# Linear attention, a gated network and a soft mixture of experts on one core: the gate's activation in one ScalarE instruction, and low parts moved from GpSimd to VectorE

## The chip, the cores and the metric

The kernel runs on one core of a Trainium2 chip. A core has a matrix engine (TensorE, PE in the profile, PEld for its weight loads), a vector engine (VectorE, DVE), an engine for functions and copies (ScalarE, ACT), a general engine (GpSimd, POOL) and a queue that issues DMAs (SyncE, SP). Each takes its instructions in order and waits for the others by semaphores. SBUF is the working memory on the chip, PSUM the banks that TensorE writes to. The metric is the device time of one execution in microseconds (us), the median of several runs.

## The reference

A softmax linear attention gives x of 2304 tokens by 512. A gated network with root-mean-square norm follows, and a mixture of eight experts, each weighted by a Sinkhorn-normalized router:

```python
def _moe_ref(x, w_gate, w_val, w_out, rms_g):          # 512 -> 1536 -> 512
    rms = np.sqrt(np.mean(x * x, axis=-1, keepdims=True) + 1e-06)
    xn = x / rms * rms_g
    g = xn @ w_gate
    silu = g * (1.0 / (1.0 + np.exp(-g)))
    val = xn @ w_val
    return (silu * val @ w_out).astype(np.float32)

def _moe2_ref(x, w_gate, w1, w2):                      # 8 experts, 512 -> 1024 -> 512
    ...                                                # P: 8 Sinkhorn steps over x @ w_gate
    for e in range(E):
        h = np.maximum(x @ w1[e], 0.0)
        out += P[:, e:e + 1] * (h @ w2[e])
```

All arrays are 32-bit floats. The change lies in the gated network alone.

## The kernel before

**Split operands.** TensorE multiplies with fp32r operands. To keep precision each operand is held as a high part (a cast by ScalarE) and a low part (value minus high part, a subtraction on VectorE or GpSimd), and a product is three matmuls: high by high, high by low, low by high (`mm3`). So every value that becomes an operand costs a cast and a subtraction, the "low part" of the change's title.

**Tiling.** The 2304 tokens are five blocks b: four of 512 and a fifth of 256 (the tails). The 1536 hidden features are twelve tiles f of 128. A product of one tile with one block accumulates in a PSUM bank.

**Features 0 to 5, plain products** (until about 330 us). `BLOCKS` is two groups: features 0 to 3 run while the attention of the later blocks is still computed, features 4 and 5 after that (from about 250 us). For each block and feature `m1_s1` forms g in a bank `pg`, then the activation, then val in a bank `pv`, multiplies (L835), and splits h (cast L837 on ScalarE, low part L838 on GpSimd). `m1_s2` multiplies h with w_out into four banks `y`, two features later in the queue, and `m1_evac` adds the banks to `acc` in SBUF (L868). The activation is silu(g) = g / (1 + exp(-g)) = 0.5 g (1 + tanh(g/2)): ScalarE forms tanh (L830), VectorE computes (tanh + 1) * g (L831), and the factor 0.5 is left to L864, L866, L868 and L1280, which take y out.

**Features 6 to 11, fast products** (about 330 to 570 us). Pairs of blocks, (0, 1) and (2, 3), are multiplied as a 2 by 2 block matrix with seven products instead of eight. `chain(f, p, gap, work)` does this for one feature f and one pair p: M1, M2, M6, M5, M7, M3, M4 in this order, three banks (x, y and then another y), sums out of them, two gates and two vals. First all features run with pair 0 (with `chain_tails` for the tails after each), then all with pair 1. `gap(k)` puts the products with w_out between (`y_gap`, added by L1280), `work(k)` other work: in pair 0 the next features' weights (`pass_tick`), in pair 1 work of the experts. In the order of the program, with the engine:

- M1 into x; ScalarE copies it to `m1` (L1202, tile `cm`). M6 is added into the same bank x, so M6 waits for that copy. `held` is emptied here: the split of the previous chain's second block is issued right after the copy of M1.
- M2 into y, M6 into x; VectorE m1 += y (L1210); ScalarE copies x to `u1` (L1211, `cu`; M7 waits for it) and forms tanh of m1 (L1212).
- M5 into a new y; VectorE (tanh + 1) * m1 (`silu`, L1188); ScalarE copies y to `m5` (L1219, `c5`; M3 waits for it).
- M7 into x; VectorE m5 += x (L1223; M4 waits for it).
- M3 into y; VectorE u1 += y (L1227); ScalarE tanh of u1 (L1229).
- M4 into x; VectorE th0 *= x (L1233), `silu` of u1 (L1188), split of the first block (cast L1192, low part on GpSimd L1193), th1 *= m5 (L1236); the split of the second block goes to `held`.

The tiles `cm`, `cu`, `c5` and the tails' `tt` take turns in three buffers (`c_tile`), so each waits for the last reader of the one before it in its buffer.

**Weights and sums of pairs.** `pass_tick` runs the JOBS: `convert` ("f", "o") turns raw weights, loaded as pairs of 32-bit words, into floats (L1006, L1007 on ScalarE, L1011, L1012, L1015 on VectorE), casts them (L1030, L1032), makes the low parts (L1033, L1043, L1054 on GpSimd) and for "f" the four sums of weight blocks (L1037 to L1041) with their split (L1044, L1047). It stores the result with a DMA of SP (L1050, L1056). `pair_sums` ("t") makes T1 to T4 of a pair of x blocks with their splits (cast L1081, low part L1085: T1 and T2 on GpSimd, T3 and T4 on VectorE); those of pair 1 are stored by SP (L1087). The tails' result of each feature is stored too (L2103), and SP's queue issues the next raw weights behind it.

The experts follow (from about 555 us): the same scheme with 32 units for each of three groups of tokens, TensorE busy nearly all the time. Their router needs one Exp on ScalarE (L936, at 594 us).

## Time and profile before

| what | value |
|---|---|
| median of 3 runs | 2021.13 us (2021.10 to 2022.15) |
| profiled execution, own time | 2021.51 us |
| its span, first to last instruction | 2019.7 us |
| TensorE busy | 1980.9 us, 98% |
| VectorE busy | 1664.8 us, 82% |
| ScalarE busy | 841.2 us, 42% |
| GpSimd busy | 196.8 us, 10% |
| mean granted TensorE clock | 0.999 |

The span is what the traces show; the device time has some 1.8 us around it. The page of a profile gives busy times and a chain of what ended last; the trace behind it can be asked for groups of instructions, for waits (who waited for whom and how long), for stretches of time and for the instructions in order. Matmuls are pipelined, one of 512 columns lasts about 0.39 us but the next starts 0.23 us after it, so TensorE's busy time is a union and a wait is what is left between.

### The profile page before, as it was taken

Reading aid. Unit: us, or ns where it says so; the run is one execution under the profiler, and the core shown is the slowest. Engines: PE = TensorE matmul, PEld = TensorE weight load, DVE = VectorE, ACT = ScalarE, POOL = GpSimd, SP = SyncE. Lnnn points to the kernel's source line nnn. Section 1 sums busy time; section 2 is a strip of 40 time slices with the busy share of each in tenths; the row PEclk is TensorE's granted clock in tenths of the full one; section 3 lists DMA queues with packets and bytes.
Section 4 is the critical chain, followed back from the end, with each engine's and each line's share of the span. In section 5 each row is a group of like instructions: output and inputs, shape, how many; then the busy total and the mean of one; then the engine's idle time right before and its main releaser. Section 6 shows DMA issues by size and latency. Waiting matters only on the chain.

```text
span 2019.7 us, 29232 instructions
## 1 busy us (share of the span) xinstructions
PE 1980.9 (98%) x10765; PEld 1836.3 (91%) x10765; DVE 1664.8 (82%) x3253; ACT 841.2 (42%) x1656; POOL 196.8 (10%) x189
## 2 busy tenths in 40 slices
PE   8899999899999999999999999999999999999999
PEld 7788887678778889998999999999999999999998
DVE  7865688867668878777778999999998899999898
ACT  5544434443445555454444333333334333333332
POOL 3532233321220000000000000000000000000000
PEclk9999999999999999999999999999999999999999
DMA  8410114468648888787978766777665777667663
GB/s 264 133 31 22 53 74 159 182 266 314 215 162 290 291 331 304 299 294 287 343 278 296 263 261 259 260 263 263 257 260 206 299 259 259 259 259 261 257 251 121
DMA packets 148838, 474.90 MB, mean 235 GB/s; under 512 B 12872, under 2 KB 77528, under 8 KB 144472
## 3 DMA queue, kind: packets, MB, share of 16 engines
q1 hardware_dynamic: 148424, 472.92, 64.1%
q8 instruction: 84, 1.38, 0.3%
q14 instruction: 58, 0.48, 0.1%
q10 hardware_dynamic: 272, 0.13, 0.0%
HBM read 331.50 MB, written 141.50 MB: 234 GB/s over the span
## 4 chain that ended last, share of the span: by engine, by line
PE 84%; DVE 8%; ACT 2%; issue 2%; POOL 1%; DMA 0%; ACTq 0%; SPq 0%; DVEq 0%; POOLq 0%
PE sb L1602 34%; PE sb L1848 13%; PE yb L1848 9%; PE yb L1637 4%; PE yb L1636 4%; PE yb L1635 4%; PE cx L1173 2%; PE pv L798 1%; PE pg L798 1%; PE cz L1173 1%; PE pg L800 1%; PE pv L799 1%; PE pv L800 1%; PE pg L799 1%; PE kv L455 1%
## 5 line engine op out<-in xcount | busy, mean ns | idle before, releaser
L1602 PE MATMUL sb<-op1T,u 128*128 128x384 f32 x1536 | 298.2, 335 | 0.1
L1865 DVE TENSOR_TENSOR acc<-sb,acc 128x384 f32<-128x384 f32 x480 | 260.6, 557 | 27.4 <-PE sb L1848 23.3
L1602 PEld LDWEIGHTS sb<-op1T,u 128*128 128x128 f32 x1536 | 269.3, 188 | 0.7 <-DVE op1T L1535 0.4
L1602 PE MATMUL sb<-op1B,u 128*128 128x384 f32 x1120 | 220.2, 334 | 0.0
L1602 PEld LDWEIGHTS sb<-op1B,u 128*128 128x128 f32 x1120 | 196.3, 188 | 0.4 <-DVE fx L1792 0.3
L1602 PE MATMUL sb<-op0T,u 128*128 128x384 f32 x768 | 149.9, 336 | 2.3 <-DVE cs L1677 1.1
L1602 PEld LDWEIGHTS sb<-op0T,u 128*128 128x128 f32 x768 | 135.5, 188 | 9.8 <-DVE cs L1677 2.6
L1792 DVE TENSOR_TENSOR fx<-mt,sb 128x384 f32<-128x384 f32 x128 | 71.0, 555 | 52.1 <-ACT mt L1796 31.2
L1602 PE MATMUL sb<-op0B,u 128*128 128x384 f32 x576 | 111.1, 336 | 0.0
L1848 PE MATMUL sb<-hc,u 128*128 128x384 f32 x504 | 104.6, 335 | 0.1
L1602 PEld LDWEIGHTS sb<-op0B,u 128*128 128x128 f32 x576 | 101.7, 188 | 2.8
L1848 PE MATMUL sb<-hd,u 128*128 128x384 f32 x492 | 102.1, 334 | 0.2 <-ACT acc L1863 0.2
L1848 PE MATMUL yb<-hd,u 128*128 128x384 f32 x426 | 96.7, 334 | 0.0
L1848 PEld LDWEIGHTS sb<-hc,u 128*128 128x128 f32 x504 | 88.7, 188 | 0.9 <-DVE acc L1865 0.6
L1848 PEld LDWEIGHTS sb<-hd,u 128*128 128x128 f32 x492 | 86.6, 188 | 0.7 <-ACT acc L1863 0.5
L1637 PE MATMUL yb<-u,hq 128*128 128x512 f32 x192 | 76.2, 397 | 0.7 <-DVE hq L1623 0.7
L1796 ACT COPY mt<-sb 128x384 f32<-128x384 f32 x64 | 30.8, 481 | 109.5 <-PE sb L1602 109.5
L1848 PEld LDWEIGHTS yb<-hd,u 128*128 128x128 f32 x426 | 75.9, 188 | 0.0
L1636 PE MATMUL yb<-u,hw 128*128 128x512 f32 x192 | 75.6, 394 | 0.0
L1637 PE MATMUL yb<-u,hw 128*128 128x512 f32 x192 | 75.6, 394 | 0.0
L1636 PE MATMUL yb<-u,hq 128*128 128x512 f32 x192 | 75.1, 391 | 0.0
L1747 DVE SCALAR_TENSOR_TENSOR fx<-fx,pb 128x384 f32<-128x384 f32 x128 | 71.3, 557 | 4.4
(472 smaller groups left out, 4613.0 us busy)
## 6 DMA issues: line engine op xcount, KB each, us to landing
u<-kept SPq DMA_DIRECT2D x256, 896.0 KB, 6.2
kept<-u SPq DMA_DIRECT2D x60, 896.0 KB, 6.0
kept<-u SPq DMA_DIRECT2D x58, 768.0 KB, 4.8
rw<-in_moe_w_dram SPq DMA_DIRECT2D x64, 512.0 KB, 5.9
pw<-w SPq DMA_DIRECT2D x12, 1024.0 KB, 4.4
w<-pw SPq DMA_DIRECT2D x12, 1024.0 KB, 7.7
kept<-u SPq DMA_DIRECT2D x58, 128.0 KB, 4.6
k<-in_k_dram SPq DMA_DIRECT2D x8, 512.0 KB, 4.4
```

Source lines behind the costliest of these rows:

```text
L798: nc.tensor.matmul(o, lhsT=w(0), rhs=xb[0], start=first, stop=False)
L799: nc.tensor.matmul(o, lhsT=w(0), rhs=xb[1], start=False, stop=False)
L800: nc.tensor.matmul(o, lhsT=w(1), rhs=xb[0], start=False, stop=last)
L1173: nc.tensor.matmul(bank, lhsT=Wf[f][wz][:, at], rhs=block_x(p, xname, xz, c), start=(start and c == 0 and j == 0), stop=(c == 1 and j == 2 ...
L1602: nc.tensor.matmul(bank[:, 0:NT], lhsT=w[wz][:, WI[wname], c, :], rhs=x[xz][c], start=(start and c == 0 and j == 0), stop=(c == 1 and j == 2),
L1635: nc.tensor.matmul(py, lhsT=h[:, 0, s], rhs=w2[0][:, d], start=(u == 0 and f == 0), stop=False)
L1636: nc.tensor.matmul(py, lhsT=h[:, 0, s], rhs=w2[1][:, d], start=False, stop=False)
L1637: nc.tensor.matmul(py, lhsT=h[:, 1, s], rhs=w2[0][:, d], start=False, stop=(u == UE - 1 and f == 1))
L1747: nc.vector.scalar_tensor_tensor(out=fb[name], in0=c, scalar=0.0, in1=pbc[g, e][z], op0=ALU.max, op1=ALU.mult,)
L1792: add = lambda o, a, b: nc.vector.tensor_tensor(out=o, in0=a, in1=b, op=ALU.add)
L1848: nc.tensor.matmul(bank[:, 0:NT], lhsT=w[wz][:, d], rhs=h[:, hz], start=(start and k == 0), stop=True, skip_group_check=True)
L1865: nc.vector.tensor_tensor(out=a, in0=bank[:, 0:NT], in1=a, op=ALU.add)
```

## The change

Three things. (a) From feature 4 on ScalarE computes Silu itself (one instruction in place of tanh on ScalarE and (tanh + 1) * g on VectorE); the factor 0.5 goes from L868 (features 4 and 5) and from L1280, which become plain sums. Features 0 to 3 keep the old form. (b) In `convert` of kind "f" the second low part (L1043) and in `pair_sums` the low parts of T1 and T2 (L1085) move from GpSimd to VectorE (`tt` is VectorE's tensor_tensor). (c) In `chain` the low part of the second block moves to VectorE; the first block's stays on GpSimd.

```diff
--- before.py
+++ after.py
@@ -827,10 +827,13 @@
         n = ntok(b)
         pg = s1_project("g", f, b, tick)
         th = tp.tile([P, 512], F32, tag="th", name=f"th{f}_{b}")
-        nc.scalar.activation(out=th[:, 0:n], in_=pg[:, 0:n], func=AF.Tanh, scale=0.5)
-        nc.vector.scalar_tensor_tensor(
-            out=th[:, 0:n], in0=th[:, 0:n], scalar=1.0, in1=pg[:, 0:n], op0=ALU.add, op1=ALU.mult
-        )
+        if f < BLOCKS[0][1]:
+            nc.scalar.activation(out=th[:, 0:n], in_=pg[:, 0:n], func=AF.Tanh, scale=0.5)
+            nc.vector.scalar_tensor_tensor(
+                out=th[:, 0:n], in0=th[:, 0:n], scalar=1.0, in1=pg[:, 0:n], op0=ALU.add, op1=ALU.mult
+            )
+        else:
+            nc.scalar.activation(out=th[:, 0:n], in_=pg[:, 0:n], func=AF.Silu)
         pv = s1_project("v", f, b, tick)
         nc.vector.tensor_tensor(out=th[:, 0:n], in0=th[:, 0:n], in1=pv[:, 0:n], op=ALU.mult)
         h = hp.tile([P, 2, 512], F32R, tag="h", name=f"h{f}_{b}")
@@ -865,9 +868,7 @@
             elif t == 0:
                 nc.vector.tensor_scalar(out=av[:, j, :], in0=py[j][:, 0:n], scalar1=0.5, scalar2=None, op0=ALU.mult)
             else:
-                nc.vector.scalar_tensor_tensor(
-                    out=av[:, j, :], in0=py[j][:, 0:n], scalar=0.5, in1=av[:, j, :], op0=ALU.mult, op1=ALU.add
-                )
+                nc.vector.tensor_tensor(out=av[:, j, :], in0=py[j][:, 0:n], in1=av[:, j, :], op=ALU.add)
 
     LX = {}
 
@@ -1040,7 +1041,7 @@
             tt(out=sums[:, 2], in0=a11, in1=a21, op=ALU.subtract)
             tt(out=sums[:, 3], in0=a12, in1=sums[:, 1], op=ALU.subtract)
             sums = sums.rearrange("p k n -> p (k n)")
-            nc.gpsimd.tensor_tensor(out=o[1][1], in0=mf[1], in1=o[0][1].bitcast(F32), op=ALU.subtract)
+            tt(out=o[1][1], in0=mf[1], in1=o[0][1].bitcast(F32), op=ALU.subtract)
             cp(out=W[0][:, 1024:2048], in_=sums)
             yield
             after()
@@ -1081,8 +1082,7 @@
                 cp(out=home(name, 0), in_=v)
 
             def low(name, v):
-                eng = nc.gpsimd if name in ("T1", "T2") else nc.vector
-                eng.tensor_tensor(out=home(name, 1), in0=v, in1=f32(home(name, 0)), op=ALU.subtract)
+                tt(out=home(name, 1), in0=v, in1=f32(home(name, 0)), op=ALU.subtract)
                 if job[1] and name != "T1":
                     nc.sync.dma_start(out=t_view(pt[name])[:, :, c], in_=f32(stage[name]))
 
@@ -1184,13 +1184,10 @@
     def c_tile(name):
         return tp.tile([P, 512], I32, tag="m", name=name, bufs=3).bitcast(F32)
 
-    def silu(th, src, n=512):
-        nc.vector.scalar_tensor_tensor(out=th[:, 0:n], in0=th[:, 0:n], scalar=1.0, in1=src, op0=ALU.add, op1=ALU.mult)
-
-    def h_split(f, b, v):
+    def h_split(f, b, v, eng):
         hpass[f, b] = h = hp.tile([P, 2, 512], F32R, tag="h", name=f"h{f}_{b}")
         nc.scalar.copy(out=h[:, 0], in_=v)
-        nc.gpsimd.tensor_tensor(out=h[:, 1], in0=v, in1=h[:, 0].bitcast(F32), op=ALU.subtract)
+        eng.tensor_tensor(out=h[:, 1], in0=v, in1=h[:, 0].bitcast(F32), op=ALU.subtract)
 
     def chain(f, p, gap, work):
 
@@ -1209,12 +1206,11 @@
         chain_product(f, p, "M6", x, False)
         tt(out=m1, in0=m1, in1=y, op=ALU.add)
         nc.scalar.copy(out=u1, in_=x)
-        nc.scalar.activation(out=th[0], in_=m1, func=AF.Tanh, scale=0.5)
+        nc.scalar.activation(out=th[0], in_=m1, func=AF.Silu)
         gap(1)
         work(1)
         y = psum(f"cz{f}_{p}")
         chain_product(f, p, "M5", y, True)
-        silu(th[0], m1)
         m5 = c_tile(f"c5{f}_{p}")
         nc.scalar.copy(out=m5, in_=y)
         gap(2)
@@ -1226,15 +1222,14 @@
         chain_product(f, p, "M3", y, False)
         tt(out=u1, in0=u1, in1=y, op=ALU.add)
         th.append(tp.tile([P, 512], F32, tag="th", name=f"tc{f}_{b1}"))
-        nc.scalar.activation(out=th[1], in_=u1, func=AF.Tanh, scale=0.5)
+        nc.scalar.activation(out=th[1], in_=u1, func=AF.Silu)
         gap(4)
         work(4)
         chain_product(f, p, "M4", x, False)
         tt(out=th[0], in0=th[0], in1=x, op=ALU.mult)
-        silu(th[1], u1)
-        h_split(f, b0, th[0])
+        h_split(f, b0, th[0], nc.gpsimd)
         tt(out=th[1], in0=th[1], in1=m5, op=ALU.mult)
-        held.append(lambda: h_split(f, b1, th[1]))
+        held.append(lambda: h_split(f, b1, th[1], nc.vector))
 
     def chain_tails(f):
 
@@ -1254,8 +1249,7 @@
                         skip_group_check=True,
                     )
         th = c_tile(f"tt{f}")
-        nc.scalar.activation(out=th[:, 0:256], in_=bank[:, 0:256], func=AF.Tanh, scale=0.5)
-        silu(th, bank[:, 0:256], 256)
+        nc.scalar.activation(out=th[:, 0:256], in_=bank[:, 0:256], func=AF.Silu)
         tt(out=th[:, 0:256], in0=th[:, 0:256], in1=bank[:, 256:512], op=ALU.mult)
         return th[:, 0:256]
 
@@ -1277,7 +1271,7 @@
     def y_add(b, j, bank):
         n = ntok(b)
         av = acc[b].rearrange("p a n -> p (a n)")[:, j * n : j * n + 512]
-        nc.vector.scalar_tensor_tensor(out=av, in0=bank, scalar=0.5, in1=av, op0=ALU.mult, op1=ALU.add)
+        nc.vector.tensor_tensor(out=av, in0=bank, in1=av, op=ALU.add)
 
     ystay = {}
 
```

## Rows read from the trace of the kernel before

**Rows 1.** The page, part 1: busy us, share of the span, instructions.
```profile
PE 1980.9 (98%) x10765; PEld 1836.3 (91%) x10765; DVE 1664.8 (82%) x3253; ACT 841.2 (42%) x1656; POOL 196.8 (10%) x189
```

**Rows 2.** Stretches: length, busy us (instructions) by engine, PE clock, DMA share, GB/s.
```profile
285.00:310.00 25.00, 22.11 (x96) 17.68 (x95) 23.65 (x31) 6.98 (x12) 12.04 (x8) 1.00 0.06 22
...
330.00:348.00 18.00, 15.63 (x85) 13.67 (x84) 16.79 (x26) 7.83 (x13) 5.27 (x4) 0.91 0.62 219
348.00:370.00 22.00, 18.88 (x94) 15.17 (x92) 17.82 (x26) 12.90 (x23) 7.11 (x5) 1.00 0.44 162
...
580.00:2019.70 1439.70, 1433.84 (x7889) 1378.86 (x7887) 1242.18 (x2481) 576.13 (x1161) 7.87 (x11) 1.00 0.73 268
```

**Rows 3.** Waits of TensorE, 255 to 580 us: total us, times, longest us.
```profile
PE cx L1173 <- DVE c L1223: 5.6, 5, 2.4
PE cx L1173 <- ACT cm L1202: 3.1, 3, 1.4
PE y L798 <- DVE acc L868: 2.9, 2, 2.2
PE cz L1173 <- ACT c L1219: 2.0, 2, 1.3
PE cx L1173 <- ACT cu L1211: 0.8, 2, 0.5
PE sb L1602 <- DVE cs L1677: 0.7, 1, 0.7
PE yr L799 <- POOL h L1193: 0.7, 2, 0.4
...
```

**Rows 4.** VectorE in order: start us, us, line, operation, tiles, shapes [idle before <-releaser].
```profile
286.07 1.77 DVE L1090 TENSOR_TENSOR s01r<-x,x 128x512 f32<-128x512 f32 x1
...
351.53 1.12 DVE L1011 TENSOR_SCALAR rf<-rf 128x512 int32<-128x512 int32 x1 [1.73 <-ACT cf L1006]
...
358.21 1.40 DVE L1038 TENSOR_TENSOR rf<-rf,cf 128x256 f32<-128x256 f32 x1
...
360.14 0.41 DVE L1040 TENSOR_TENSOR rf<-cf 128x256 f32<-128x256 f32 x1
...
369.48 1.65 DVE L1236 TENSOR_TENSOR tc<-tc,c 128x512 f32<-128x512 f32 x1
```

**Rows 5.** Groups on VectorE, 255 to 580 us: count | busy us, mean ns | idle before.
```profile
L1188 DVE SCALAR_TENSOR_TENSOR tc<-tc,cu 128x512 f32<-128x512 f32 x12 | 9.2, 768 | 0.3 <-ACT tc L1229 0.3
L1188 DVE SCALAR_TENSOR_TENSOR tc<-tc,cm 128x512 f32<-128x512 f32 x12 | 8.2, 682 | 3.3 <-ACT tc L1212 3.3
...
L831 DVE SCALAR_TENSOR_TENSOR th<-th,pg 128x512 f32<-128x512 f32 (+1 forms) x10 | 6.3, 631 | 9.4 <-ACT th L830 9.4
...
L1188 DVE SCALAR_TENSOR_TENSOR tt<-tt,ct 128x256 f32<-128x256 f32 x6 | 2.5, 414 | 2.3 <-ACT tt L1257 2.3
...
L1085 DVE TENSOR_TENSOR gT<-s11q,gT 128x512 fp32r<-128x512 f32 x2 | 1.4, 684 | 0.0
```

**Rows 6.** Groups on GpSimd, 255 to 580 us.
```profile
L1193 POOL TENSOR_TENSOR h<-tc,h 128x512 fp32r<-128x512 f32 x24 | 35.8, 1502 | 115.8 <-ACT h L1192 93.1 <-PE cx L1173 14.2 <-issue 7.7
...
L1043 POOL TENSOR_TENSOR w<-cf,w 128x512 fp32r<-128x512 f32 x6 | 8.3, 1383 | 2.6 <-ACT w L1032 2.6
```

**Rows 7.** TensorE in order: the tail matmuls of features 6 and 8.
```profile
344.11 4.29 PE L1248 MATMUL ct<-x,w 128*128 128x256 f32 x24
...
386.65 3.04 PE L1248 MATMUL ct<-x,w 128*128 128x256 f32 x24
```

**Rows 8.** ScalarE: the only table load (ns min/median/max, start), then instructions in order.
```profile
L1971 ACT ACT_TABLE_LOAD  x1: 1283/1283/1283, 1.2 to 1.2; - x1
...
365.88 0.63 ACT L1229 ACTIVATE tc<-cu 128x512 f32<-128x512 f32 x1 [1.56 <-DVE cu L1227]
...
368.38 0.62 ACT L1192 CAST h<-tc 128x512 fp32r<-128x512 f32 x1
...
369.53 0.59 ACT L1202 COPY cm<-cx 128x512 f32<-128x512 f32 x1 [0.26 <-DVE tc L1188]
```

## What the change should do to the time

> **What bounds the kernel now.** I read the page first: TensorE is busy 98% of the span [rows 1], so only its idle time can be won. The table by stage says where that idle time lies [rows 2]: in 580 to 2019.7 us TensorE misses 5.9 us of 1439.7, but in 285 to 310 it misses 2.9 of 25, in 330 to 348 2.4 of 18 and in 348 to 370 3.1 of 22. In just these stretches VectorE is busiest, 23.7 of 25, 16.8 of 18 and 17.8 of 22 us. They belong to the gated network, which the diff touches. Then the list of waits of TensorE from 255 to 580 us [rows 3]: 17.6 us in all. It waits 5.6 us for VectorE's sum L1223 (M4 needs its bank back), 3.1 for the copy L1202 (M6), 2.9 for L868 (banks of y), 2.0 for L1219 (M3), 0.8 for L1211 (M7), 0.9 for GpSimd's low parts (0.7 of it in the row shown), and 2.3 in four waits where the last network starts, the largest 0.7. The timeline of VectorE in feature 7 [rows 4] shows why: L1038, a subtraction of 256 columns, takes 1.40 us where L1040, the same shape, takes 0.41; L1011 takes 1.12 and L1236 1.65. Beside each of the long ones GpSimd runs a subtraction of its own, 1.38 to 1.50 us in the mean [rows 6]. VectorE's queue is late, and TensorE waits for what stands at its end.
>
> **What the change removes and adds on VectorE.** It removes ten L831 (6.3 us) and thirty L1188 (9.2, 8.2 and 2.5): 26.2 us [rows 5]. It adds 26 low parts: six in `convert` (L1043), eight in `pair_sums` (T1 and T2), twelve in `h_split` (second block of a pair). On VectorE such a subtraction takes 0.684 us when nothing is beside it [rows 5]: 17.8 us. Busy time falls by 8.4 us, and with the 26 GpSimd instructions go long ones beside them, some 1.0 us each (L1038 1.40 against 0.41; L1090, beside a T2 low part, 1.77 against 0.68) [rows 4, 5]. L868 and L1280 become plain sums without the 0.5; the two kinds of instruction cost the same here (0.682 and 0.684 us for 512 columns, rows 5), so nothing.
>
> **What it changes on ScalarE.** Silu replaces Tanh one for one, forty times, on the same tile, in the same place of the queue. Tanh took 0.63 us where a cast of the same size took 0.62 [rows 8]: ScalarE's time here goes by size, so I take no difference, and 0.01 us each, 0.4 in all, as the bound either way. One table load is in the trace, 1.28 us at the start, and Exp, Tanh, Abs, Square and Copy all run on it [rows 8]. Silu needs another before feature 4, and the router's single Exp a third. The first comes where ScalarE waits for TensorE's pg, and no wait of TensorE in rows 3 is at pg; the other stands past 580 us, where ScalarE works 576 of 1440 us [rows 2]. I cost both at 0; uncovered they are 2.6 us.
>
> **The waits, one by one.**
>
> (1) L868, 2.9 us in two waits [rows 3]. Ahead of each in VectorE's queue stand the sums of half a pair. Per half pair two L831 go (1.26), two long instructions shorten (2.1, by the L1090 row), two low parts come (1.37): 2.0 us earlier. The first wait, 0.7, goes, of the second, 2.2, about 2.0: 2.7.
>
> (2) L1223, 5.6 us in five: 2.4 in feature 6, 1.2 each in 7 and 9, 0.4 each in 8 and 10. In feature 7, ahead of it on VectorE, L1011 loses 0.7 and L1038 1.0, one L1188 goes and one low part comes (0.7 each): 1.7 us earlier. But M3 in front of M4 moves 0.75 by (3), so 0.9 is left each for 7 and 9, which run alike. In 6 the first part is held by the landing of the next weights: 0.8. In 8 and 10 the 0.4 go. Together 0.8 + 1.8 + 0.7 (the two are 0.35 each): 3.3.
>
> (3) L1219, 2.0 us in two. On ScalarE it stands behind the cast L1032, which waits for VectorE's conversion. That starts with L1011, 1.12 us, beside GpSimd's split of the second block. VectorE now does that split itself, in the 1.73 us in which it waits for ScalarE anyway [rows 4], and L1011 takes 0.4: 0.75 each, 1.5.
>
> (4) L1202, 3.1 us in three. The tile `cm` shares three buffers with `cu`, `c5` and `tt`; the new one waits for L1188, the last reader of the old `cu` [rows 8]. With the change that reader is ScalarE's own Silu, long done. This frees 0.26 [rows 8]; the cast ahead waits for L1233, which comes 2.0 us earlier while TensorE is 1.4 ahead: another 0.3 to 0.6. Of 3.1 I take 1.7, 0.57 each.
>
> (5) L1211, 0.8 in two. It stands behind a weight conversion that waits for a load, which SP issues after the tail's store, which waits for L1259. Ahead of L1259 L1188 leaves twice (0.77 and 0.41) and L1236 shortens by 1.0: all 0.8.
>
> (6) GpSimd's low parts, 0.9: half are now VectorE's, 0.68 for 1.50 us: 0.5. The last network's start, 2.3: L1188 leaves the queue ahead of its first sum, and a low part with its wait enters: 0.
>
> (7) TensorE's clock. After the wait of 2.4 us in feature 6 the 24 tail matmuls took 4.29 us, against 3.04 in feature 8 [rows 7], and the stage's mean clock is 0.91 [rows 2]: for a part of it 1.2 instead of 2.4 GHz. In feature 7, with waits up to 1.4 us, the clock is 1.00 [rows 2, 3]. With the long wait at 1.6 I take 1.25, here 1.3, as won; the bound below is 0.
>
> The sum: 2.7 + 3.3 + 1.5 + 1.7 + 0.8 + 0.5 + 1.3 = 11.8 us. Past 580 us TensorE has next to no idle time, so what is won before stays. The profiled execution took 2021.5 us (span 2019.7 and 1.8 around it), against a median of 2021.1; 2021.5 - 11.8 = 2009.7.
>
> **The rivals.**
>
> The held split blocks VectorE. The second block's low part now stands in VectorE's in-order queue ahead of the next feature's conversions, and waits for ScalarE's cast, which stands behind the copy of M1. For it: `held` splits and conversions meet at the start of every feature. Against it: VectorE idles 1.73 us at that place already [rows 4]. If it costs 0.7 us in seven of the twelve waits of (2) to (5), 4.9 of their 7.3 us are lost: 2021.5 - 6.9 = 2014.6. Chance 0.18.
>
> VectorE stops being the bound. Shifts add up from feature to feature, and all waits but those of the last network's start go: 15.3 and 1.3 us: 2004.9. Chance 0.1.
>
> The table loads are not covered: two of 1.28 us delay a copy that TensorE waits for: 2012.3. For it: a load holds ScalarE, and TensorE's waits include its copies [rows 3]. Against it: neither stands where TensorE waits. Chance 0.07. The Trainium skill, "ScalarE: Activation LUTs" (What ACT_TABLE_LOAD costs), gives about 2.66 us for each switch of set, a drain included, and its Rules say to group activations by set, which speaks against this change. By it the two would be 5.3 us and the time 2015.0, an estimate from that page; the trace agrees on the load alone (1283 ns), no row shows a drain.
>
> The change doesn't release what TensorE waits for. ScalarE's own order of casts and copies holds M3, M6 and M4, and only (1) goes: 2018.8, within 0.2%. Chance 0.07.
>
> The tables alternate. If Silu's set lacked Abs or Copy, ScalarE would load before each of a feature's three Silus and again before the conversions. In the five features with conversions three loads each stand ahead of copies that TensorE waits for: 15 times 1.28 is 19.2, less 11.8: 2028.9, slower. It decides from the tenth load on the path (11.8 / 1.28). Against it: the one load in the trace serves five functions [rows 8]. Chance 0.04. By the same page (Table sets: the hidden batching unit) abs, copy, relu and identity are in every set; the trace agrees for the one set that it shows.
>
> **How the numbers follow.** Forecast 0.54, rivals 0.18, 0.1, 0.07, 0.07 and 0.04. A measurement of this kernel can tell some 0.2%, 4 us, from no change. The forecast and the first three rivals are faster, 0.89; a tail of 0.03 of them ends over 2017.1: faster 0.86, same 0.10, slower 0.04. The range reaches down to the rival in which all waits go, 2004.5, and up past the held split and the uncovered loads to 2016.5, which also holds a clock that falls as before (1.3 us) together with half of (2) lost (1.7).
>
> **What would show it.** Right: L1236, L1038 and L1011 at 0.69, 0.42 and 0.42 us; TensorE's wait for L868 under 0.5 us and for L1223 near 2.3; clock 1.00 in the stage of feature 6; three table loads. Wrong: VectorE waiting over 1 us longer at the second block's low part, with conversions behind it; more than three loads; L1236 still at 1.65, which leaves 1 us a feature on the path.

## The result and the profile after

The changed kernel takes 2004.94 us in the median of four runs (2004.67 to 2005.19), the one before 2021.64 (2021.1 to 2023.06) beside it: ratio 0.9916, 95% interval 0.9899 to 0.9933, or 16.7 us less. The forecast was 2009.7, inside its range of 2004.5 to 2016.5, but only 0.4 above the lower end: the direction and the places were right, the gain of 11.8 us was too small by 4.9.

The page, part 1, of the kernel after (busy us, share, instructions):

```profile
PE 1975.4 (99%) x10765; PEld 1835.0 (92%) x10765; DVE 1638.9 (82%) x3239; ACT 843.0 (42%) x1658; POOL 156.8 (8%) x163
```

Against [rows 1] VectorE lost 25.9 us, GpSimd 40.0, ScalarE gained 1.8 and TensorE, with the same 10765 matmuls, lost 5.5. The span went from 2019.7 to 2002.6.

Where in the span it went shows in one stretch. It begins with the gate projection of feature 3 on the fourth block, 28 us ahead of feature 4, in work that the change doesn't touch, and ends with the first matmul of the last network (the experts). The table by stretches (length, then busy us by engine as in [rows 2]); before:

```profile
223.10:554.60 331.50, 316.27 (x1571) 261.80 (x1571) 248.19 (x371) 137.34 (x246) 98.53 (x67) 0.99 0.50 187
...
344.10:363.00 18.90, 16.97 (x79) 14.12 (x78) 14.90 (x21) 9.62 (x17) 5.74 (x4) 0.92 0.47 169
363.00:386.60 23.60, 21.60 (x103) 17.20 (x102) 18.94 (x29) 10.30 (x20) 8.35 (x6) 1.00 0.60 224
```

and the same three stretches after:

```profile
222.40:537.30 314.90, 311.52 (x1571) 261.26 (x1571) 223.39 (x358) 137.90 (x247) 60.13 (x42) 1.00 0.53 197
...
338.50:354.60 16.10, 15.73 (x79) 12.86 (x78) 11.99 (x20) 10.36 (x18) 3.03 (x2) 1.00 0.56 204
354.60:375.90 21.30, 20.91 (x104) 17.45 (x103) 16.98 (x28) 10.38 (x19) 6.26 (x4) 1.00 0.65 236
```

The stretch is 16.6 us shorter, which is all of the gain. Of that 11.85 is idle time of TensorE (331.50 less 316.27, against 314.90 less 311.52), and 4.75 is busy time: the same 1571 matmuls take less. The second and third row are features 7 and 8, each from the tail matmuls of the feature before to its own. In 7 the busy time falls by 1.24 as the clock goes from 0.92 to 1.00. In 8 it falls by 0.69 although the clock was 1.00 both times.

Waits of TensorE, 255 to 580 us, after (total us, times, longest us):

```profile
PE cx L1173 <- DVE c L1219: 2.3, 4, 1.1
PE cx L1173 <- ACT cm L1199: 0.8, 2, 0.4
PE sb L1596 <- DVE cs L1671: 0.7, 1, 0.7
...
```

With three of the last network's start that are left out here (0.6, 0.4, 0.4) they come to 5.2 us, where [rows 3] had 17.6. The lines moved: L1219 here is the sum L1223 of before, L1199 the copy L1202. The waits for L868, for the copy L1219 of before, for L1211 and for GpSimd's low parts are gone.

VectorE in feature 7 (start us, us, line, operation, tiles), which answers [rows 4]:

```profile
344.17 0.69 DVE L1190 TENSOR_TENSOR h<-tc,h 128x512 fp32r<-128x512 f32 x1 [1.68 <-ACT h L1189]
344.78 0.42 DVE L1012 TENSOR_SCALAR rf<-rf 128x512 int32<-128x512 int32 x1
...
349.35 1.40 DVE L1038 TENSOR_TENSOR rf<-cf 128x256 f32<-128x256 f32 x1
```

L1012 (L1011 before) is down from 1.12 to 0.42, and the added low part, L1190, stands where VectorE idled before. But one subtraction of the conversion still takes 1.40.

TensorE's tail matmuls of feature 6, against [rows 7], take full-speed time:

```profile
338.51 3.04 PE L1243 MATMUL ct<-x,w 128*128 128x256 f32 x24
```

And ScalarE's two added table loads, in order of time, against [rows 8]:

```profile
253.59 1.28 ACT L836 ACT_TABLE_LOAD   x1 [2.19 <-PE pg L800]
254.88 0.60 ACT L836 ACTIVATE th<-pg 128x512 f32<-128x512 f32 x1
...
576.00 0.52 ACT L1613 ACTIVATE hq<-cs 128x384 fp32r<-128x384 f32 x1
576.54 1.28 ACT L937 ACT_TABLE_LOAD   x1
577.83 0.32 ACT L937 ACTIVATE probs<-probs 128x144 f32<-128x144 f32 x1
```

### The profile page after: what moved, and what is told of

The parts are those of the page before. It is cut to its first block, busy times and chain, and to the rows that moved or that the text cites. A ratio compares the mean times of both kernels' runs of the same rounds, so it can differ in the third digit from the quotient of the medians.

```text
span 2002.6 us, 29166 instructions
## 1 busy us (share of the span) xinstructions
PE 1975.4 (99%) x10765; PEld 1835.0 (92%) x10765; DVE 1638.9 (82%) x3239; ACT 843.0 (42%) x1658; POOL 156.8 (8%) x163
## 3 DMA queue, kind: packets, MB, share of 16 engines
HBM read 331.50 MB, written 141.50 MB: 236 GB/s over the span
## 4 chain that ended last, share of the span: by engine, by line
PE 90%; DVE 4%; ACT 1%; issue 1%; DMA 1%; POOL 0%; ACTq 0%; DVEq 0%; SPq 0%
PE sb L1596 34%; PE sb L1842 13%; PE yb L1842 10%; PE yb L1631 4%; PE yb L1630 4%; PE yb L1629 4%; PE cx L1173 2%; PE pv L798 1%; PE pv L800 1%; PE pv L799 1%; PE pg L798 1%; PE y L798 1%; PE y L800 1%; PE y L799 1%; PE pg L800 1%; PE pg L799 1%
## 5 line engine op out<-in xcount | busy, mean ns | idle before, releaser
L1630 PE MATMUL yb<-u,hw 128*128 128x512 f32 x192 | 75.6, 394 | 0.0
L1631 PE MATMUL yb<-u,hw 128*128 128x512 f32 x192 | 75.6, 394 | 0.0
L1629 PE MATMUL yb<-u,hw 128*128 128x512 f32 x192 | 74.9, 390 | 0.0
```

What stands on the lines that cost most here:

```text
L1629: nc.tensor.matmul(py, lhsT=h[:, 0, s], rhs=w2[0][:, d], start=(u == 0 and f == 0), stop=False)
L1630: nc.tensor.matmul(py, lhsT=h[:, 0, s], rhs=w2[1][:, d], start=False, stop=False)
L1631: nc.tensor.matmul(py, lhsT=h[:, 1, s], rhs=w2[0][:, d], start=False, stop=(u == UE - 1 and f == 1))
```

## The experiments

An execution's whole time also carries what happens before the change. In the traces of `low_alone`, `no_held` and `no_pair` TensorE's clock falls to half at 26 us and at 67 us, and the stretch starts at 225.1 us; in the other traces, which have no fall at 26 us, it starts at 222.4 to 223.1. So beside the time the table gives the length of the stretch above, from the one trace of each kernel. The 109 us ahead of the stretch, the same work in all 14 kernels, take 108.94 to 108.96 us in every trace, so a difference of some tenths in the stretch is the kernel's. Run next to the kernels of the table, the kernel before took 2021.3 to 2022.5 us in the median.

| kernel | median us | runs | stretch us |
|---|---|---|---|
| before | 2021.64 | 4 | 331.5 |
| after | 2004.94 | 4 | 314.9 |
| silu_alone | 2010.05 | 5 | 318.6 |
| low_alone | 2019.65 | 11 | 326.4 |
| no_held | 2007.84 | 5 | 317.3 |
| no_pair | 2005.94 | 5 | 315.4 |
| no_conv | 2005.42 | 1 | 316.1 |
| reader | 2007.25 | 1 | 316.2 |
| late6 | 2008.93 | 1 | 318.4 |
| late7 | 2007.76 | 1 | 317.9 |
| tables | 2026.48 | 1 | 336.6 |
| sum_first | 2005.09 | 5 | 314.6 |
| first_too | 2009.39 | 1 | 317.8 |
| conv_both | 2004.28 | 5 | 313.5 |

### Either part alone

`silu_alone`, against the kernel after: ScalarE's Silu, with all low parts where they were.

```diff
-            tt(out=o[1][1], in0=mf[1], in1=o[0][1].bitcast(F32), op=ALU.subtract)
+            nc.gpsimd.tensor_tensor(out=o[1][1], in0=mf[1], in1=o[0][1].bitcast(F32), op=ALU.subtract)
...
-                tt(out=home(name, 1), in0=v, in1=f32(home(name, 0)), op=ALU.subtract)
+                eng = nc.gpsimd if name in ("T1", "T2") else nc.vector
+                eng.tensor_tensor(out=home(name, 1), in0=v, in1=f32(home(name, 0)), op=ALU.subtract)
...
-        held.append(lambda: h_split(f, b1, th[1], nc.vector))
+        held.append(lambda: h_split(f, b1, th[1], nc.gpsimd))
```

> Only the Silu on ScalarE (with the 0.5 left out); all 26 low parts stay on GpSimd. Theory (VectorE's queue sets TensorE's waits; both parts shorten it): the long VectorE instructions beside GpSimd stay (L1038 and L1011 over 1 us), the wait for the copy cast L1219 of before (M3) stays near 2 us, the wait for the sum that frees M4's bank falls from 5.6 to about 3, the wait for y's banks goes: 2012 to 2013 us, about half of the gain. Rival 1 (only the instructions that Silu removes count, the moved low parts cost VectorE what they give back): 2005, like the whole change. Rival 2 (the relief of GpSimd is what counts): 2017 or more.

`low_alone`, against the kernel after: the 26 low parts on VectorE, with Tanh, the `silu` instructions and the factor 0.5 as before, at all of their places.

```diff
-        nc.scalar.activation(out=th[0], in_=m1, func=AF.Silu)
+        nc.scalar.activation(out=th[0], in_=m1, func=AF.Tanh, scale=0.5)
...
+        silu(th[0], m1)
...
```

> Only the 26 low parts moved to VectorE; tanh and the product on VectorE stay. Theory: VectorE's busy time rises by 18 us less some 20 us of waiting beside GpSimd that goes; L1011 and L1038 at 0.42 us; TensorE's wait for M3 goes, for M4's bank falls from 5.6 to near 4, for M6 stays near 3 since the tile of the old u1 is still read by VectorE: 2013 us. Rival 1 (moved low parts are an even trade): 2021. Rival 2 (the relief of GpSimd is what counts): 2007 or less.

Silu alone took 2010.05 us, ratio 0.9938 (0.9926 to 0.995); the low parts alone 2019.65, ratio 0.9989 (0.998 to 0.9998). In the stretch Silu alone wins 12.9 us, the low parts alone 5.1, together 16.6: they overlap by 1.4. Silu alone won more than was expected of it (2012 to 2013 us), the low parts alone much less (2013): their time is nearer to the rival of an even trade (2021). What each does to the engines shows in the stretch's row. Silu alone:

```profile
222.80:541.40 318.60, 311.99 (x1571) 261.01 (x1571) 223.68 (x333) 137.12 (x247) 94.93 (x67) 1.00 0.52 194
```

Low parts alone:

```profile
225.20:551.60 326.40, 315.50 (x1572) 261.86 (x1572) 247.93 (x397) 137.91 (x246) 64.38 (x42) 0.99 0.51 190
```

VectorE is busy 248.19 us before, 223.68 with Silu alone and 247.93 with the low parts alone. Silu takes 24.5 us off it. The 26 low parts add 17.8 of their own (26 x 0.684, rows 5, an estimate) and save as much in neighbours that GpSimd lengthened: 0.3 us off in the balance, not the extra relief that the prediction's "1.0 us each" implied (by the same estimate 0.7 each instead). What they win, they win by where they stand in the queue.

The low parts' 5.1 us do not reach the end: the whole time falls by 2.0. The last network starts behind a longer wait, for `cs`, in the kernel with the low parts alone:

```profile
557.76 1.37 PE L1601 MATMUL sb<-op0T,u 128*128 128x384 f32 x6 [2.05 <-DVE cs L1676]
```

In before the longest wait at this place was 0.7 [rows 3]. VectorE in order shows what stands ahead of L1676 now, the last low part and its wait:

```profile
556.55 0.69 DVE L1192 TENSOR_TENSOR h<-tc,h 128x512 fp32r<-128x512 f32 x1 [0.68 <-ACT h L1191]
557.16 0.55 DVE L1676 TENSOR_TENSOR cs<-mc,sb 128x384 f32<-128x384 f32 x1
```

The granted clock then falls to half at 559 us for 3.4 us, and from the last network's first matmul to the end it takes 1468.5 us where before took 1465.1. The prediction expected this entry (step 6: a low part and its wait enter VectorE's queue, L1188 leaves it): with Silu in, the balance is 0, without it 3.4 us. This is the trace of a run of 2021.85 us. Not every run need have lost so much: four of the eleven took 2017.4 to 2018.8 at a mean clock of 0.999, the other seven 2019.3 to 2022.4 at 0.996 or 0.997.

### Each low part put back

`no_held` (second block's split back on GpSimd), `no_pair` (T1 and T2 back), `no_conv` (the conversion's L1044 back), each on the kernel after:

```diff
-        held.append(lambda: h_split(f, b1, th[1], nc.vector))
+        held.append(lambda: h_split(f, b1, th[1], nc.gpsimd))
```

> The whole change, but the low part of the second block of each pair stays on GpSimd. Theory (VectorE had idle time at that place, and GpSimd's subtraction there lengthens the first conversion instruction by 0.7 us): the waits for M3 and for GpSimd's low parts come back in part, 2006.5 to 2008. Rival (the split blocks VectorE's in-order queue while it waits for ScalarE, 12.5 us of waiting in the trace): faster than the whole change, 2002 to 2004.

```diff
-                tt(out=home(name, 1), in0=v, in1=f32(home(name, 0)), op=ALU.subtract)
+                eng = nc.gpsimd if name in ("T1", "T2") else nc.vector
+                eng.tensor_tensor(out=home(name, 1), in0=v, in1=f32(home(name, 0)), op=ALU.subtract)
```

> The whole change, but the low parts of T1 and T2 stay on GpSimd. Theory: with Silu's instructions gone VectorE has room in that stage, the wait for y's banks comes back by 0 to 1 us: 2005 to 2006. Rival (the moved low parts carry that stage's gain of 3 us): 2007.5 or more.

```diff
-            tt(out=o[1][1], in0=mf[1], in1=o[0][1].bitcast(F32), op=ALU.subtract)
+            nc.gpsimd.tensor_tensor(out=o[1][1], in0=mf[1], in1=o[0][1].bitcast(F32), op=ALU.subtract)
```

> The change with the six low parts of `convert` (L1044) back on GpSimd. Of the 3.7 us by which the change beats Silu alone between feature 4 and the last network's start, the second block's split gave 2.4 and the pair's low parts 0.5. Theory (the three moves add up): 0.8 is left for this one, so 315.7 us for that stretch where the change has 314.9, and L1219's waits grow by 0.1 to 0.2 in each odd feature. Rival (it stands ahead of L1219 on VectorE, so GpSimd's slow low part lengthens what is beside it by 0.6 in each of six features, all on TensorE's path): 317.5 or more. Rival (it cost VectorE as much as it gave): 314.5 to 315.0.

The stretch grows by 2.4, 0.5 and 1.2 us: 4.1 in sum, where Silu alone lacks 3.7. So the three are close to independent, and twelve of the 26 carry over half. With T1 and T2 back (`no_pair`) no wait for L871 (L868 before) returns; the wait for the sum in feature 6 grows from 1.14 to 1.51. Without the second block's split on VectorE, TensorE waits for the copy L1215 again:

```profile
PE cx L1173 <- DVE c L1219: 1.9, 4, 1.1
PE cz L1173 <- ACT c L1215: 1.4, 2, 0.7
...
```

That is the chain of step (3), and it is the rival "the held split blocks VectorE" turned round: the split on VectorE does wait for ScalarE (12.5 us in 11 waits), and is worth 2.4 us all the same. What it costs is small: with the split back on GpSimd TensorE's waits for the sum in features 6, 7 and 9 stay at 1.14, 0.28 and 0.28, and one in the second pair falls from 0.57 to 0.25. The row, of the kernel after, waits of VectorE:

```profile
DVE h L1190 <- ACT h L1189: 12.5, 11, 1.7
```

For `no_conv`, theory 315.7, rivals 317.5 or 315.0 at most, measured 316.1: nearest to the sum. The place was half as expected. The wait for L1219 grows in features 7 and 9, by 0.4 each (from 0.28 and 0.29 to 0.66), but falls by 0.6 in feature 6 (from 1.14 to 0.54), so that its total stays at 2.3; the 1.2 us come by `cm`, 0.6 more in each of features 8 and 10.

```profile
PE cx L1173 <- DVE c L1219: 2.3, 4, 0.7
PE cx L1173 <- ACT cm L1199: 2.0, 2, 1.0
```

### How late VectorE may be

`late6` puts four multiplications of `m5` by 1 (0.42 us each) ahead of the sum in feature 6, first pair; `late7` three of them in each of features 7 to 10.

```diff
+        if f == F0 and p == 0:
+            for _ in range(4):
+                nc.vector.tensor_scalar(out=m5, in0=m5, scalar1=1.0, scalar2=None, op0=ALU.mult)
```

> The whole change, with four multiplications of m5 by 1 (0.42 us each, some 1.3 us in VectorE's queue) ahead of the sum that frees M4's bank in feature 6 of pair 0, so that TensorE's wait there goes from 1.1 to about 2.4 us, as long as before the change. Theory (the fall of TensorE's clock before the change followed from that wait): the clock falls to half after it, the tail matmuls take over 4 us, and the kernel loses 1.3 and some 1.5 more: 2.7 to 3.2 us of stage time. Rival (the fall has another cause): the clock stays, 1.3 us.

```diff
+        if F0 < f < F1 and p == 0:
+            for _ in range(3):
+                nc.vector.tensor_scalar(out=m5, in0=m5, scalar1=1.0, scalar2=None, op0=ALU.mult)
```

> The change with three multiplications of `m5` by 1 (0.42 us each, 1.27 together) ahead of the sum m5 += x in features 7 to 10 of the first pair. Theory (VectorE's queue is what TensorE waits for at M4 only in the features that still show a wait, 0.3 us in 7 and 8, and in 9 and 10 it is within a few tenths of it): TensorE's wait for this sum grows by 1.0 to 1.3 in each of the four, 4 to 5 us, with the clock at full speed since no wait comes to 2 us; the stretch from feature 4 to the last network becomes 319 to 320.5. Rival (VectorE has slack where feature work is not beside it, in 8 and 10): only 7 and 9 grow, 2 to 2.6 us, and the stretch is 317 to 317.6. Rival (VectorE is no longer the bound at all): under 1 us.

In `late6` the wait in feature 6 goes from 1.14 to 3.05 us, 1.9 more, but the stretch grows by 3.5, a little over the theory's 2.7 to 3.2. TensorE in order, then the stretch around it:

```profile
339.60 2.43 PE L1173 MATMUL cx<-pT,w 128*128 128x512 f32 x6 [3.05 <-DVE c L1222]
```

```profile
325.00:345.00 20.00, 16.95 (x89) 14.62 (x88) 15.08 (x27) 7.80 (x13) 2.69 (x2) 0.91 0.51 192
```

The clock is 0.91 in these 20 us, half speed for 3.4 us, and the remaining 1.6 us are its price: what step (7) put at 1.3.

In `late7` only 7 and 9 grow, by 1.5 and 1.6 us, 8 and 10 by nothing: 317.9, close to the first rival (317 to 317.6), and not the theory (319 to 320.5). The total of TensorE's wait for the sum:

```profile
PE cx L1173 <- DVE c L1222: 5.3, 4, 1.7
```

So after the change VectorE still bounds features 6, 7 and 9, where a delay of 1.27 costs TensorE 1.5 of waiting (0.28 to 1.74 in feature 7), and has at least 1.27 us of slack at this sum in 8 and 10. No wait came to 2 us, and the clock stayed at 1.00.

### The sum ahead of the queue's other work

`sum_first`, on the kernel after: in the first pair the conversion's step that stood ahead of the sum is issued behind it.

```diff
-        work(2)
+        if p:
+            work(2)
         chain_product(f, p, "M7", x, False)
         tt(out=m5, in0=m5, in1=x, op=ALU.add)
+        if p == 0:
+            work(2)
```

> The whole change, and in pair 0 the sum that frees M4's bank (m5 += M7) is issued ahead of work(2) instead of behind it, so that conversions no longer stand before it in VectorE's queue. Theory (what is left of TensorE's waits, 2.3 us for this sum, is that queue's order): these waits go with 0.3 us of refill each, 2001.5 to 2003. Rival (VectorE then stands idle waiting for M7 with the conversions behind it, and the waits for M3 and M6 grow): 2005 or more.

2005.09 us, ratio 0.9915 (0.9902 to 0.9929), stretch 314.6: the theory's gain of 2 to 3 us did not come, the rival's time did. The wait moved:

```profile
PE cx L1173 <- ACT cm L1199: 3.1, 2, 1.6
...
PE cx L1173 <- DVE c L1220: 0.4, 1, 0.4
```

The sum's wait falls from 2.3 to 0.4, and `cm`, which ScalarE copies behind the casts that need the now later conversion, rises from 0.8 to 3.1. So this change of order wins nothing; that what is left is the amount of work of VectorE and ScalarE between two features is a reading of it, not shown.

### The buffer of `cu`

`reader`, on the kernel after: one column of `cu` is multiplied by 1 where L1188 stood, so that the buffer that `cm` takes over has a late reader on VectorE again.

```diff
+        if p == 0:
+            nc.vector.tensor_scalar(out=u1[:, 0:1], in0=u1[:, 0:1], scalar1=1.0, scalar2=None, op0=ALU.mult)
         h_split(f, b0, th[0], nc.gpsimd)
```

> The change with one more instruction of VectorE per feature in the first pair, where L1188 stood: it multiplies one column of `cu` by 1 in place, so that `cu`'s buffer has a late reader on VectorE again, at next to no busy time (under 0.1 us each). Theory of step (4) (part of the gain at the copy `cm` is that its buffer no longer waits for VectorE): TensorE's waits for `cm` rise from 0.8 us in two to 1.3 to 1.6 in two or three, and the stretch from feature 4 to the last network by 0.5 to 1.0 us, to 315.4 to 315.9. Rival (the earlier release of ScalarE's cast was the whole of it): waits for `cm` stay at 0.8 and the stretch at 314.9 within 0.3.

The wait for `cm` rose from 0.8 to 2.0 and the stretch by 1.3, more than the theory's 0.5 to 1.0; yet the theory is not borne out. In feature 8 the wait stayed at 0.39; all of the rise is in feature 10, and ScalarE did not idle ahead of the copy there. The three engines in order, of `reader`:

```profile
395.92 1.29 POOL L1034 TENSOR_TENSOR wo<-co,wo 128x512 fp32r<-128x512 f32 x1 [7.62 <-ACT wo L1031]
396.22 1.54 DVE L1016 CUSTOM_DVE_ANT_0 co<-ro,co 128x1024 uint16<-128x1024 uint16 x1 [0.49 <-ACT wo L1031]
...
397.79 0.62 ACT L1033 CAST wo<-co 128x512 fp32r<-128x512 f32 x1 [1.95 <-DVE co L1016]
...
399.19 0.58 ACT L1199 COPY cm<-cx 128x512 f32<-128x512 f32 x1
```

and the same place in the kernel after:

```profile
395.44 0.69 DVE L1016 CUSTOM_DVE_ANT_0 co<-ro,co 128x1024 uint16<-128x1024 uint16 x1
395.48 1.81 POOL L1034 TENSOR_TENSOR wo<-co,wo 128x512 fp32r<-128x512 f32 x1 [7.63 <-ACT wo L1031]
...
396.16 0.62 ACT L1033 CAST wo<-co 128x512 fp32r<-128x512 f32 x1 [0.76 <-DVE co L1016]
```

The same two instructions meet. In the kernel after, VectorE starts first, takes its 0.69, and GpSimd is stretched to 1.81. In `reader` GpSimd starts first, takes 1.29, and VectorE 1.54. The cast L1033 waits for VectorE, and the copy stands behind the cast. So the buffer's reader costs nothing by itself once VectorE is early; what cost 1.2 us is who started first. How much of the old wait was the reuse, in the kernel before, this run can't tell.

### More low parts to VectorE

`first_too` also takes the first block's split to VectorE, `conv_both` the conversion's first low part (L1034, where it belongs to a feature's gate and value weights: six instructions in the trace, not the three that were expected).

```diff
-        h_split(f, b0, th[0], nc.gpsimd)
+        h_split(f, b0, th[0], nc.vector)
```

> The whole change, and the low part of the first block of each pair on VectorE too, so that GpSimd runs no split of the chain. Theory: that low part waits 0.6 us for ScalarE's cast with the product of the second block and the tails behind it, so the copy for M6 comes later: stage time 0.5 to 3 us longer. Rival (GpSimd beside VectorE is what costs): 1 to 2 us shorter.

```diff
-        nc.gpsimd.tensor_tensor(out=o[1][0], in0=mf[0], in1=o[0][0].bitcast(F32), op=ALU.subtract)
+        (nc.vector if kind == "f" else nc.gpsimd).tensor_tensor(
+            out=o[1][0], in0=mf[0], in1=o[0][0].bitcast(F32), op=ALU.subtract
+        )
```

> The change with the first low part of the conversion of a feature's weights (L1034) on VectorE too, three instructions; it is the one beside which L1038 still takes 1.40 us. Theory (as long as VectorE idles behind it and GpSimd's instruction lengthens its neighbour by 1.0, 0.68 of own work for it is a gain): 0 to 0.3 us in each odd feature, the stretch 314.0 to 314.9 and the time 2004 to 2005. Rival (it stands ahead of what TensorE waits for, as the first block's split did, and the low part has a later deadline on GpSimd): 0.3 to 0.7 us in each odd feature, 316 to 317 and 2006 to 2007.5.

`first_too` is 2.9 us longer in the stretch, as its theory had it, but at another place than expected: TensorE waits 2.6 us for `cu` in two waits and 1.5 at the last network's start. `conv_both` is 1.4 us shorter, which is more than its theory allowed, at 2004.28 us (2003.9 to 2004.87), ratio 0.9915 (0.9901 to 0.9928): the lowest time of the study, but only the stretch tells it from the change, whose runs took 2004.67 to 2005.19. Its waits:

```profile
PE cx L1175 <- DVE c L1221: 1.2, 2, 0.9
PE cx L1175 <- ACT cm L1201: 0.9, 2, 0.6
```

The waits of the sum in features 7 and 9 are gone. So whether a low part is better on VectorE is not settled by the sum of busy time, which hardly moves, but by whether GpSimd's version stands beside something that TensorE waits for (the conversion) or VectorE's delays it (the first block).

### Table loads on the path

`tables` puts an Exp of one column ahead of each of the first pair's 18 Silus: 36 more loads.

```diff
+        if p == 0:
+            nc.scalar.activation(out=warm, in_=ident[:, 0:1], func=AF.Exp)
         nc.scalar.activation(out=th[0], in_=m1, func=AF.Silu)
```

> The whole change, with an Exp of one column ahead of each of the 18 Silus of pair 0 and its tails, which makes ScalarE load a table before the Exp and before the Silu: 36 loads, 46 us of ScalarE. The rival that the tables alternate said that about half of the loads stand ahead of copies that TensorE waits for: 19 us or more, 2024. If ScalarE's idle time covers them: under 5 us, 2010 or less. If a load also drains the engine for another 1.4 us each, the gap after each load shows it.

The stretch grows by 21.7 us. The 36 loads take 46.2 us (1.283 each) and the 18 Exps 0.2 each, 50 together; some two fifths of that come through, two falls of TensorE's clock included, mostly at two places:

```profile
PE cx L1173 <- ACT cm L1199: 11.6, 5, 2.8
PE cz L1173 <- ACT c L1217: 6.1, 4, 1.8
```

The rival "the tables alternate" had its mechanism and its places (copies that TensorE waits for) right; the change escapes it because its own Silu's table also serves Abs, Copy and the casts, so that only two loads were added. The load itself ends where the next instruction begins:

```profile
348.76 1.28 ACT L1210 ACT_TABLE_LOAD   x1
350.06 0.20 ACT L1210 ACTIVATE warm<-ident 128x1 f32<-128x1 f32 x1
```

## Why the prediction was right, and which sizes were off

The mechanism was the one forecast: VectorE's queue is short enough that what stands at its end is ready, and TensorE's waits go in the gated network, with nothing given back behind it. The gain was 4.9 us larger. Term by term, from [rows 3] to the waits after:

| step | wait before | wait after | forecast | won |
|---|---|---|---|---|
| (1) L868 | 2.9 | 0 | 2.7 | 2.9 |
| (2) the sum | 5.6 | 2.3 | 3.3 | 3.3 |
| (3) the copy of M5 | 2.0 | 0 | 1.5 | 2.0 |
| (4) `cm` | 3.1 | 0.8 | 1.7 | 2.3 |
| (5) L1211 | 0.8 | 0 | 0.8 | 0.8 |
| (6) low parts; last network | 0.9; 2.3 | 0; 2.1 | 0.5; 0 | 0.9; 0.2 |
| (7) clock | | | 1.3 | 1.6 |

The waits give 12.4 for 10.5 and the clock 1.6 (the price in `late6`) for 1.3: 2.2 of the 4.9. No large term failed; (3), (4) and (6) were each taken 0.4 to 0.6 too low. In (3) and (4) the prediction counted only what is saved within the feature (0.75 and 0.57 a wait). The wait of 1.3 at M3 in feature 9 fell by over 1.0: VectorE also enters the feature earlier. That is read from the rows, not tested by a run of its own.

The other 2.7 us are a term that the sum did not have: a wait costs TensorE more than the idle time that the list shows. Feature 8 shows it without any change of clock. TensorE's waits in it, before:

```profile
370.17 1.65 PE L1173 MATMUL cx<-pT,w 128*128 128x512 f32 x6 [1.36 <-ACT cm L1202]
...
377.69 1.66 PE L1173 MATMUL cx<-pT,w 128*128 128x512 f32 x6 [0.29 <-ACT cu L1211]
...
385.16 1.66 PE L1173 MATMUL cx<-pT,w 128*128 128x512 f32 x6 [0.35 <-DVE c L1223]
```

and after:

```profile
360.81 1.65 PE L1173 MATMUL cx<-pT,w 128*128 128x512 f32 x6 [0.40 <-ACT cm L1199]
```

Idle time falls by 1.6 (2.0 to 0.4), the feature by 2.3 (23.6 to 21.3, the third rows of the tables by stretches), and the busy time of its matmuls by 0.7. Taken from the start of one matmul to the start of the next, each of these four waits lasts 0.27 us longer than its idle time: 0.16 ahead of the first matmul, 0.11 between the first and the second. The list holds 21 waits before and 10 after; eleven times 0.27 is 3.0. Two of the eleven, at M3 in features 7 and 9, are not wholly gone: they still take 0.36 each from start to start, with no idle time that the list would name. That leaves 2.3 of the 2.7 explained.

The total of (1) is right, but not by its working, which adds up three savings: with Silu alone no wait for L868 is left, with the low parts alone 1.7 us are. The total of (2) agrees partly by offset. Feature 6 kept 1.14 where 1.6 was expected, 7 and 9 kept 0.28 and 0.29 where 0.3 was expected, but a wait of 0.6 is new near 523 us, in the second pair.

The signs that the prediction named: waits for L868 at 0 (under 0.5 was asked), the sum at 2.3, three table loads, clock 1.00, L1011 at 0.42. Two were wrong. L1038 is still 1.40 in feature 7, and the last product (L1236, now L1231) is 0.77 in the mean, but 1.19 beside GpSimd in features 7 and 9. The step that failed there is "with the 26 GpSimd instructions go long ones beside them, some 1.0 us each": GpSimd keeps its other low part in every conversion (L1034), and the next instruction of VectorE that reads SBUF alone is held by it. Moved low parts took away 0.7 each, VectorE's busy time fell by 25.9 us where the prediction's terms make some 34 (8.4 and 26 times 1.0), and `conv_both`, which moves that one too, is the one addition that won.

Of the rivals, the held split is settled by `no_held` and the row of its 12.5 us: it waits, and TensorE loses at most 0.3 us by it. "VectorE stops being the bound" gives 2004.9, the time that came, but not for its reason: 3.1 us of waits for the sum and for `cm` are left, and by `late7` VectorE still bounds three features. The table loads cost nothing, as forecast, but the reason given for the first was wrong: it does not run while ScalarE waits for `pg` but behind that wait (the row at 253.59), and so holds the first Silu back by 1.28 us; no wait of TensorE follows before 337 us. The one at 576 us stands beside a last network that takes the same time as before (1465.2 against 1465.1 us). The rival that only (1) goes is out by the table above.

What stays open is how much of (4) was the reuse of `cu`'s buffer: `reader` shows that it costs nothing now, not what it cost when VectorE was late.

## What to carry to other kernels

Where one engine idles behind another's in-order queue, take work out of that queue whole (here Silu, 24.5 us and 78% of the gain) before moving it between engines that disturb each other (17.8 us of low parts moved, nothing in VectorE's busy time, 22% of the gain). Price every wait that goes with its restart, and look at each moved instruction by who stands behind it: the same kind of move won 2.4, 1.2, 0.5 and 1.4 us at four places and lost 2.9 at a fifth.

## What the runs showed of the hardware

**VectorE and GpSimd: the one that starts first takes its normal time, the other is stretched.** The kernel after, both engines in order:

```profile
358.05 0.69 DVE L1016 CUSTOM_DVE_ANT_0 co<-ro,co 128x1024 uint16<-128x1024 uint16 x1
358.09 1.81 POOL L1034 TENSOR_TENSOR wo<-co,wo 128x512 fp32r<-128x512 f32 x1 [7.62 <-ACT wo L1031]
358.66 0.68 DVE L1229 TENSOR_TENSOR tc<-tc,cx 128x512 f32<-128x512 f32 x1
359.26 1.19 DVE L1231 TENSOR_TENSOR tc<-tc,c 128x512 f32<-128x512 f32 x1
...
369.04 1.29 POOL L1034 TENSOR_TENSOR w<-cf,w 128x512 fp32r<-128x512 f32 x1 [5.74 <-issue]
369.15 1.72 DVE L1016 CUSTOM_DVE_ANT_0 cf<-rf,cf 128x1024 uint16<-128x1024 uint16 x1
```

At 358 VectorE is 0.04 us ahead and keeps its 0.69; at 369 it is 0.11 behind and takes 1.72, ending 0.54 after GpSimd. L1229, which reads the bank `cx`, takes 0.68 in the middle of GpSimd's 1.81; L1231, which reads two tiles of SBUF, ends 0.55 after GpSimd. So the price is what is left of GpSimd's instruction when VectorE's arrives, up to 1.0 us, and only for some instructions; the flat 1.0 of the prediction was its upper end. The Trainium skill, "SBUF — State Buffer" (SBUF: two separate sides), says that the shared pair of ports is an exclusive lock for the whole instruction, taken by whichever starts first, and that a VectorE instruction with two SBUF inputs competes for it; the trace agrees, by these rows.

**A change of ScalarE's table costs the load and no more.** 1.283 us, begun 0.02 us after the last instruction before it and followed within 0.02 by the next one (rows at 576 and in `tables`). The Trainium skill, "ScalarE: Activation LUTs" (What ACT_TABLE_LOAD costs), has about 2.66 us with a drain; no run here shows a drain.

**TensorE's clock fell to half after some long waits and not after others.** It fell for 3.4 us after waits of 2.05 (twice in `low_alone`), 2.37 (before) and 3.05 (`late6`), and the price measured by itself is 1.6 us (`late6`). In this stretch no shorter wait of any kernel was followed by a fall, but the length of the wait alone doesn't decide: the clock stayed at full speed after the 2.2 at L868 [rows 2, 3], and in `tables` two of four waits of the same length (2.70 to 2.76) were followed by slow matmuls (2.42 and 2.36 for six, against 1.67). One of each, TensorE in order:

```profile
365.79 2.42 PE L1173 MATMUL cx<-pT,w 128*128 128x512 f32 x6 [2.70 <-ACT cm L1199]
...
391.44 1.67 PE L1173 MATMUL cx<-pT,w 128*128 128x512 f32 x6 [2.74 <-ACT cm L1199]
```

Nor does the kernel's work alone decide: a wait of 2.06 to 2.10 us for GpSimd's L368, at 64 to 66 us, stands in all 14 traces, ahead of everything that the kernels differ in, and the clock fell 1.1 to 1.4 us after it in seven of them and not in the other seven. So a fall can come in one execution and not in another of the same work, and the 1.6 us of step (7) need not be lost in every run of the kernel before. What decides stays open.
